# Seven products of quarters in place of eight for a 512-row channel matmul, with the sums on VectorE and GpSimd

## The chip, the cores and the metric

The kernel runs on one core of a Trainium2 chip. The metric is device time in microseconds (us), the median over executions.

Five engines take part. TensorE ("PE" in the profile) multiplies, and its weight loads have a line of their own ("PEld"). VectorE ("DVE"), ScalarE ("ACT") and GpSimd ("POOL") work element by element. SyncE ("SP") does nothing here but issue transfers, which run on 16 DMA engines. Each engine has its own queue of instructions; in these traces it works through it in order (group 3 below shows sums on VectorE that stand behind an operation which waits for a load). SBUF is the on-chip memory, and PSUM the one that TensorE's products go to.

## The reference

```python
# q, k, v: (8 batches, 8 heads, 576 rows, 64), float32
theta = pi / 2 * arange(576) / 576
phi(x) = concat([relu(x) * cos(theta), relu(x) * sin(theta)], axis=-1)     # 128 features
kv  = einsum('bhsf,bhsd->bhfd', phi(k), v);   z = phi(k).sum(axis=2)
x   = einsum('bhsf,bhfd->bhsd', phi(q), kv) / (einsum('bhsf,bhf->bhs', phi(q), z) + 1e-6)
x   = x as (8, 576, 512)
u   = x + (relu(x^T @ w_tok1) @ w_tok2)^T          # tokens: 576 -> 256 -> 576
out = u + relu(u @ w_ch1) @ w_ch2                  # channels: 512 -> 1536 -> 512
```

The last line is the largest part. The change concerns its second product, `relu(u @ w_ch1) @ w_ch2`.

## The kernel before

All inputs of the matmuls are bf16, sums on TensorE are fp32. The rows of the channel part are worked on in 8 "groups" of 512 rows that matter here, one per batch for batches 1 to 7 (g = 1..7), and g = 8 for the tails, which are the last 64 rows of all eight batches. Batch 0 is done in the head of the kernel, which also casts weights and is not pipelined in this way.

In group g TensorE does 48 matmuls for the first channel product (12 tiles of `h1T`, 4 matmuls each), then 48 for the second (4 row tiles, 12 matmuls each). Each is 128x128 weights against 512 columns.

```python
def mlp1(g, mi):                      # first channel matmul, one of 12 tiles
    ps = nextM()
    for ki in range(NCC):             # 4
        nc.tensor.matmul(ps..., wc1[:, ki, mi*P:(mi+1)*P], src[:, :, ki, :], ...)
    return ps

def mlp2(g, t, part, ps, sub=(0, 4)):  # second channel matmul, a third of one row tile
    for ki in range(4 * part + sub[0], 4 * part + sub[1]):
        nc.tensor.matmul(ps, h1T[:, ki, t * P:(t + 1) * P], wc2[:, ki, :],
                         start=(ki == 0), stop=(ki == NCH - 1))

def mlp2_out(g, t, ps, last):
    nc.vector.tensor_add(r[:, t % 2, :], ps, group(g)[1][:, t, :])     # + u
    stores.append(lambda: store(g, t, r))
```

Between these 24 steps of a group the rest of the work is interleaved: attention and token part of batch b = g+1, and features of batch f = g+2, with the loads for the batch after that at the end.

```python
def plan_of(g):
    b, f = g + 1, g + 2
    ...                                       # [cut: g == 1 has its own plan]
    if b < B:
        for j in range(NJ):  put(2 + j, num_step, b, j)      # attention output, wants qpT
        for n in range(2):
            put(8 + n, b1_step, b, n)                        # token matmul 1
            put(11 + n, u_step, b, n)                        # token matmul 2, u, u's transpose (DMA)
        put(13, tail_step, b)
    if f < B:
        for j in range(NJ):
            put(7 + j, k_step, f, j)          # key features (VectorE, ScalarE), value cast (GpSimd)
            put(12 + 2 * j, q_step, f, j)     # query features, then a transpose by DMA into qpT
            put(18 + j, kv_step, f, j)        # k^T v on TensorE
    if f + 1 < B:
        put(NS - 1, loads_step, f + 1)        # k, v, q of one batch: 3.54 MB
```

Loads, the five query transposes and the two or three transposes of u in a group are all issued by SyncE, so they stand in one queue. The stores go through GpSimd's queue, those of the tails through SyncE's and ScalarE's.

Of the kernel before, what the change touches and what calls it, by code (L numbers as in the profile page):

```python
# [18 lines left out]
def kernel(  # L19
# [11 lines left out]
    nc = tc.nc  # L31
# [24 lines left out]
    def sb(name, shape, dt):  # L56
        return const.tile(shape, dt, name=name)
# [27 lines left out]
    h1T = sb("h1T", [P, NCH, 4 * P], BF16)  # L85
    res_all = sb("res", [P, 2, 2, Dm], F32)
    res = [res_all[:, i] for i in range(2)]
    wz = sb("wz", [P, 512], BF16)

    LO, HI = slice(0, P // 2), slice(P // 2, P)  # L90
    psM, psA = [], []
# [2 lines left out]
    def nextM():  # L94
        cnt["M"] += 1
        return psM[(cnt["M"] - 1) % 4]
# [3 lines left out]
        return psA[cnt["A"] % 2]  # L100


    def place(b, j):
        return j

    def load(b, src, name, engs, h0=0, h1=None):
        h1 = H if h1 is None else h1
        dst = raw[name][b % 2]
        s = src[b].rearrange("h (i n) d -> i h n d", n=9)
        parts = ((1, 5, 9, 0), (0, 0, 5, 0))  # L110
        for (par, lo, hi, at), eng in zip(parts, engs):
            eng.dma_start(out=dst[par:P:2, h0:h1, at:at + hi - lo, :], in_=s[:, h0:h1, lo:hi, :])


    def feat(eng, out_ap, in_ap, tab, j):
        s = tab[:, j:j + 1]
        if eng is nc.scalar:
            eng.activation(out_ap, in_ap, AF.Relu, bias=0.0, scale=s)  # L118
        else:
            eng.tensor_scalar(out_ap, in_ap, scalar1=s, scalar2=0.0, op0=ALU.mult, op1=ALU.max)  # L120

    def kfeat(b, j, e0, e1, h0=0, h1=H):
        src = raw["k"][b % 2][:, h0:h1, place(b, j), :]
        feat(e0, kp[j][:, h0:h1, 0, :], src, cos_t, j)
        feat(e1, kp[j][:, h0:h1, 1, :], src, sin_t, j)

    def qfeat(b, j, e0, e1, h0=0, h1=H):
        src = raw["q"][b % 2][:, h0:h1, place(b, j), :]
        feat(e0, qp[j][:, h0:h1, 0, :], src, cos_t, j)
        feat(e1, qp[j][:, h0:h1, 1, :], src, sin_t, j)  # L130

    def copy(eng, out_ap, in_ap):
        if eng is nc.scalar:
            eng.copy(out_ap, in_ap)
        else:
            eng.tensor_copy(out_ap, in_ap)  # L136

    def vcast(b, j, eng, h0=0, h1=H):
        copy(eng, vb[j][:, h0:h1, 0:D], raw["v"][b % 2][:, h0:h1, place(b, j), :])

    def qturn_dma(b, j):
        nc.sync.dma_start_transpose(out=qpT[:, :, j, :],
# [158 lines left out]
    def mlp1_part(g, mi, bank, kis):  # L301
        src = group(g)[0]
        for ki in kis:
            nc.tensor.matmul(bank.rearrange("p (t k) -> p t k", k=P), wc1[:, ki, mi * P:(mi + 1) * P],
                             src[:, :, ki, :], start=(ki == 0), stop=(ki == NCC - 1))
# [12 lines left out]
    def mlp2_out(g, t, ps, last):  # L318
        r = res[(t // 2) % 2]
        nc.vector.tensor_add(r[:, t % 2, :], ps, group(g)[1][:, t, :])  # L320
        stores.append(lambda: store(g, t, r))

    stores = []

    def flush():
# [31 lines left out]
                nc.tensor.transpose(t[:, i, h, :], qp[j][:, HH * hf + h, :, :].rearrange("p a d -> p (a d)"),  # L357
                                    ident)

    def turn_half_out(hf, js, bank, eng):  # L360
        t = bank.bitcast(BF16).rearrange("p (j h t) -> p j h t", j=2, h=HH)
        dst = qpT[:, HH * hf:HH * hf + HH, js[0]:js[0] + len(js), :].rearrange("p h j t -> p j h t")
        copy(eng, dst, t[:, 0:len(js), :, :])

    def kv_half(hf, j):
        ps = bank_kv(hf)
# [11 lines left out]
    def num_half(hf, js, ps):  # L378
        for i, j in enumerate(js):
            for h in range(HH):  # L380
                num_mm(ps[:, i, h * E1:(h + 1) * E1], HH * hf + h, j)

    def x_half(hf, js, ps, b, stages=(0, 1, 2)):
        m = len(js)
        n = ps[:, 0:m, 0:HH * E1].rearrange("p g (h e) -> p g h e", h=HH)
        r = rden[(js[0] // 2) % 2]
        rm = r[:, 0:m, :]
        if 0 in stages:
            nc.vector.tensor_scalar_add(rm, n[:, :, :, D], 1e-6)
        if 1 in stages:  # L390
            nc.vector.reciprocal(rm, rm)
        if 2 not in stages:
            return
        c0 = HH * D * hf
        if js[0] < T:
            dst = x_sb[:, js[0]:js[0] + m, c0:c0 + HH * D].rearrange("p g (h d) -> p g h d", h=HH)
        else:
            dst = x_tl[b % 2][:, c0:c0 + HH * D].rearrange("p (g h d) -> p g h d", g=1, h=HH)
        rb = bass.AP(tensor=r.tensor, offset=r.offset, ap=[r.ap[0], [HH, m], [1, HH], [0, D]])
        nc.vector.tensor_mul(dst, n[:, :, :, 0:D], rb)  # L400

    def b1_half(hf, js, bank, b):
        c0 = HH * D * hf
        for j in js:
            for mi in range(NT):
                ks = slice(0, P) if j < T else LO
                rhs = x_sb[:, j, c0:c0 + HH * D] if j < T else x_tl[b % 2][LO, c0:c0 + HH * D]
                nc.tensor.matmul(bank[:, mi * 256:(mi + 1) * 256], w1[ks, j, mi * P:(mi + 1) * P], rhs,  # L408
                                 start=(j == 0 and mi == 0), stop=(j == NJ - 1 and mi == NT - 1),
                                 skip_group_check=True)  # L410
# [23 lines left out]
    def uT_out(b, c, bank, eng):  # L434
        copy(eng, uT[b % 2][:, :, c, :], bank.rearrange("p (t k) -> p t k", t=T))
# [112 lines left out]
    def turn(hf, i):  # L548
        turn_half(hf, pairs[i], psT[i % 2])

    def turn_o(hf, i, eng):
        turn_half_out(hf, pairs[i], psT[i % 2], eng)

    warm(12)
    for j in range(NJ):
# [33 lines left out]
        kv_half(1, j)  # L589
    turn(1, 1)  # L590
    kv_half_out(1, A)
    turn_o(1, 1, A)
    turn(1, 2)
    turn_o(1, 2, V)
    w1_cast(0, 2, G)
# [5 lines left out]
        wc1_cast(mi, G)  # L601
    for i in range(2):
        num_half(1, pairs[i], num_b[i])
    for st in range(3):
        for i in range(2):
            x_half(1, pairs[i], num_b[i], 0, (st,))
    b1_half(0, range(NJ), psK[0], 0)
    b1_half_out(0, psK[0], 0, A)
    num_half(1, pairs[2], num_b[2])
    x_half(1, pairs[2], num_b[2], 0)  # L610
    for c in range(2):
        uT_x(c, psT[c])
    b1_half(1, (0, 1), psK[1], 0)
    for c in range(2):
        uT_h(0, c, psT[c])
        uT_out(0, c, psT[c], A)
    b1_half(1, (2, 3, 4), psK[1], 0)
    b1_half_out(1, psK[1], 0, V, 0)
    b1_half_out(1, psK[1], 0, A, 1)
    bank_u = {2: psK[0], 3: psN[1][:, 0, :]}  # L620
    bank_h = {0: psT[0], 1: psT[1], 2: psN[0][:, 0, :], 3: psN[0][:, 1, :]}
    for c in (2, 3):
        uT_x(c, bank_u[c])
    for mi in (0, 1):
        mlp1_part(0, mi, bank_h[mi], (0, 1))
    for c in (2, 3):
        uT_h(0, c, bank_u[c])
        uT_out(0, c, bank_u[c], (A, V)[c - 2])
    for mi in (2, 3):
        mlp1_part(0, mi, bank_h[mi], (0, 1))  # L630
    for mi in (0, 1):
# [21 lines left out]


    def f1k(b, j, which, eng):
        feat(eng, kp[j][:, :, which, :], raw["k"][b % 2][:, :, place(b, j), :], (cos_t, sin_t)[which], j)

    for j in range(NJ):
        vcast(1, j, G)
# [85 lines left out]
        load(3, src_of[n], n, (SY, SY))  # L745


    NS = 24

    def kv_step(b, j):  # L750
        kv(b, j)
# [40 lines left out]
    def plan_of(g):  # L792
        b, f = g + 1, g + 2
        plan = [[] for _ in range(NS)]

        def put(s, fn, *args):
            plan[s].append(lambda: fn(*args))

        if g == 1:
            put(5, tail_step, 1)  # L800
            put(13, tail_turn, 1)
            for j in range(NJ):
                put(j // 2 + 1, f1k, b, j, 0, V)
                put((j + 1) // 2 + 2, kv_step, b, j)
                put(5 + j, num_step, b, j)
            put(3, u_out, 1, 1)
            for n in range(2):
                put(11 + n, b1_step, b, n)
                put(14 + n, u_step, b, n)
            for j in range(NJ):  # L810
                put(8 + j, k_step, f, j)
                put(18 + j, kv_step, f, j)
            for j, at in enumerate((12, 13, 16, 17, 18)):
                put(at, q_step, f, j)
            put(NS - 1, loads_step, 4)
            return plan
        if b < B:
            for j in range(NJ):
                put(2 + j, num_step, b, j)
            for n in range(2):  # L820
                put(8 + n, b1_step, b, n)
                put(11 + n, u_step, b, n)
            put(13, tail_step, b)
        if f < B:
            for j in range(NJ):
                put(7 + j, k_step, f, j)
                put(12 + 2 * j, q_step, f, j)
                put(18 + j, kv_step, f, j)
        if f + 1 < B:
            put(NS - 1, loads_step, f + 1)  # L830
        return plan

    for g in range(1, B + 1):
        mps = {}
        plan = plan_of(g)
        for s in range(NS):
            if s < NCH:
                ps = mlp1(g, s)
            else:
                t, part = divmod(s - NCH, 3)  # L840
                if part == 0:
                    mps[t] = nextM()
                mlp2(g, t, part, mps[t])
            for fn in plan[s]:
                fn()
            flush()
            if s < NCH:
                mlp1_out(s, ps, V if s in (7, 9, 11) else A)
            elif part == 2:
                mlp2_out(g, t, mps[t], g == B)  # L850

    flush()
    _ = tile, bass_utils
# [30 lines left out]
```

## Time and profile before

The median was 274.08 us (3 runs, 273.56 to 274.92).

A stretch from the first channel matmul of one group to that of the next: this is the windows view. Its columns are the stretch in us, its length, then the busy us and number of instructions of PE, PEld, DVE, ACT and POOL, then the granted clock, the busy share of the 16 DMA engines, and the GB/s that they moved. The rows are groups 1, 2, 3, 6 and 7.

```profile
57.50:86.90 29.40, 29.29 (x246) 14.56 (x245) 21.34 (x43) 16.29 (x26) 5.79 (x10) 1.00 0.85 233
86.90:114.90 28.00, 27.97 (x207) 13.52 (x208) 16.57 (x35) 15.70 (x25) 6.30 (x11) 1.00 0.88 228
114.90:142.10 27.20, 27.20 (x203) 13.34 (x202) 16.45 (x34) 15.04 (x24) 5.25 (x9) 1.00 0.89 237
...
197.30:224.10 26.80, 26.80 (x168) 12.27 (x167) 12.89 (x25) 9.11 (x15) 3.40 (x6) 1.00 0.38 96
224.10:244.80 20.70, 20.70 (x98) 9.38 (x97) 4.84 (x7) 5.37 (x9) 2.15 (x4) 1.00 0.13 52
```

In groups 1 to 5 (4 and 5, left out, have 0.95 and 0.87) TensorE is full and the DMA engines are at 0.85 to 0.95.

Two more readings were used for the prediction. From the timeline, first the five key features of group 1 alone, and then how such a feature runs while GpSimd is casting:

```profile
59.07 2.15 DVE L120 TENSOR_SCALAR kp<-k_raw,cos_t 128x512 bf16<-128x512 f32 x5
71.29 3.41 POOL L136 CAST vb<-v_raw 128x512 bf16<-128x512 f32 x5 [11.89 <-DMA v_raw<-in_v_dram]
71.47 0.71 DVE L120 TENSOR_SCALAR kp<-k_raw,cos_t 128x512 bf16<-128x512 f32 x1
```

The feature takes 0.43 us a piece alone (2.15 for five) and 0.71 when a GpSimd cast is under way. And from the chain of waits, the second channel product of group 7, 48 matmuls in 10.36 us (215.9 ns a piece):

```profile
234.59 10.36 PE psM L315 x48
```

### The profile page before, as it was taken

To read this page: it belongs to the slowest core of one execution; us is meant where nothing else is said; L and a number is where in the kernel's file an instruction comes from. 1 tells how busy PE (TensorE), PEld (TensorE's weight loads), DVE (VectorE), ACT (ScalarE), POOL (GpSimd) and SP (SyncE) were. 2 spreads that over 40 slices of the span, in tenths; PEclk is the share of its full clock that TensorE was granted. 3 is DMA by queue.
4 is the path that set the end of the run, shared out by engine and by line. 5 is a ranking of instruction groups with operands and counts; after the bars stand their busy time and mean duration, and the time that the engine had idled before them with its cause. 6 is when DMAs were issued, how large, how long until landed. Compare 5 with 4: busy or idle time off the path is not lost.

```text
span 270.6 us, 4991 instructions
## 1 busy us (share of the span) xinstructions
PE 259.8 (96%) x1878; PEld 127.6 (47%) x1878; DVE 150.4 (56%) x330; ACT 136.1 (50%) x223; POOL 66.7 (25%) x130
## 2 busy tenths in 40 slices
PE   7689999999999999999999999999999999999992
PEld 2465465445445544554455445544554444444440
DVE  5872856796982658366836684477446531331331
ACT  4763685874673666354745474547553405204300
POOL 4195647160401222110412041104120011011000
PEclk9999999999999999999999999999999999999999
DMA  6999999999849993999499969996890051011022
GB/s 206 368 376 391 385 393 372 257 221 331 271 89 244 274 358 70 207 242 356 148 200 211 356 187 202 219 353 190 183 216 2 22 153 79 2 78 78 0 79 80
DMA packets 79480, 57.15 MB, mean 211 GB/s; under 512 B 48224, under 2 KB 73952, under 8 KB 79456
## 3 DMA queue, kind: packets, MB, share of 16 engines
q1 hardware_dynamic: 76032, 47.39, 63.7%
q0 software_dynamic: 2560, 8.39, 9.2%
q10 hardware_dynamic: 864, 1.05, 1.2%
q8 instruction: 15, 0.25, 0.4%
q14 instruction: 9, 0.07, 0.1%
HBM read 35.85 MB, written 9.44 MB: 167 GB/s over the span
## 4 chain that ended last, share of the span: by engine, by line
PE 87%; DVE 5%; DMA 4%; ACT 1%; issue 1%; SPq 0%; DVEq 0%
PE psM L297 34%; PE psM L315 31%; PE psA L235 5%; PE psA L213 5%; PE psA L163 3%; PE psA L182 3%; DMA k_raw<-in_k_dram 2%; DMA uT<-u_bf 2%; PE psA L186 1%; PE psK L408 1%; PE psA L217 1%; PE psA L276 1%; DVE res L320 1%; DVE qp L120 1%; PE psA L149 1%
## 5 line engine op out<-in xcount | busy, mean ns | idle before, releaser
L315 PE MATMUL psM<-w_ch,h1T 128*128 128x512 bf16 x432 | 102.2, 379 | 0.0
L297 PE MATMUL psM<-uT,w_ch 128*128 128x512 bf16 x368 | 88.0, 379 | 0.7 <-DVE res L320 0.5
L309 ACT ACTIVATE h1T<-psM 128x512 bf16<-128x512 f32 x77 | 45.8, 596 | 52.1 <-PE psM L297 50.8
L315 PEld LDWEIGHTS <-h1T 128*128 128x128 bf16 x432 | 39.7, 97 | 43.9 <-issue 1.5
L297 PEld LDWEIGHTS <-w_ch 128*128 128x128 bf16 x416 | 37.8, 97 | 42.6 <-issue 2.5
L320 DVE TENSOR_TENSOR res<-psM,u_sb 128x512 f32<-128x512 f32 x32 | 22.0, 689 | 38.0 <-PE psM L315 38.0
L136 POOL CAST vb<-v_raw 128x512 bf16<-128x512 f32 (+1 forms) x43 | 24.3, 609 | 58.7 <-DMA v_raw<-in_v_dram 49.2
L118 ACT ACTIVATE kp<-k_raw,sin_t 128x512 bf16<-128x512 f32 (+1 forms) x45 | 28.1, 667 | 14.1 <-DMA k_raw<-in_k_dram 14.1
L334 POOL DMA_DIRECT2D out_dram<-res x16 | 9.0, 563 | 90.8 <-DVE res L320 90.8
L311 DVE TENSOR_SCALAR h1T<-psM 128x512 bf16<-128x512 f32 x27 | 18.5, 683 | 20.3 <-PE psM L297 20.3
L120 DVE TENSOR_SCALAR kp<-k_raw,cos_t 128x512 bf16<-128x512 f32 (+1 forms) x45 | 20.9, 500 | 9.6 <-DMA k_raw<-in_k_dram 9.6
L118 ACT ACTIVATE qp<-q_raw,sin_t 128x512 bf16<-128x512 f32 (+1 forms) x40 | 24.9, 678 | 0.0
L240 DVE TENSOR_TENSOR u_sb<-psA,x_sb 128x1024 f32<-128x1024 f32 x16 | 19.5, 1216 | 9.8 <-PE psA L235 9.8
L203 DVE TENSOR_TENSOR x_sb<-psA,rden 128x512 bf16<-128x512 f32 x28 | 19.4, 691 | 1.0
L245 ACT CAST u_bf<-u_sb 128x1024 bf16<-128x1024 f32 x12 | 12.5, 1046 | 11.8 <-DVE u_sb L240 9.1
L120 DVE TENSOR_SCALAR qp<-q_raw,cos_t 128x512 bf16<-128x512 f32 (+1 forms) x40 | 16.4, 445 | 2.0 <-DMA q_raw<-in_q_dram 2.0
L235 PE MATMUL psA<-B,w_tok 128*128 128x512 bf16 x64 | 16.4, 379 | 0.0
L163 PEld LDWEIGHTS <-kp 128*128 128x128 bf16 x280 | 12.4, 98 | 6.8
L182 PEld LDWEIGHTS <-qpT 128*128 128x128 bf16 x256 | 11.8, 98 | 8.2 <-issue 1.4
L173 ACT CAST kv_sb<-psA 128x520 bf16<-128x520 f32 x7 | 4.2, 603 | 21.0 <-PE psA L163 21.0
L213 PE MATMUL psA<-x_sb,w_tok 128*128 128x512 bf16 x56 | 14.4, 379 | 0.0
L163 PE MATMUL psA<-vb,kp 128*128 128x65 bf16 x280 | 13.3, 193 | 0.0
(108 smaller groups left out, 198.1 us busy)
## 6 DMA issues: line engine op xcount, KB each, us to landing
out_dram<-res POOLq DMA_DIRECT2D x32, 256.0 KB, 3.7
k_raw<-in_k_dram SPq DMA_DIRECT2D x7, 640.0 KB, 8.3
v_raw<-in_v_dram SPq DMA_DIRECT2D x7, 640.0 KB, 9.8
q_raw<-in_q_dram SPq DMA_DIRECT2D x7, 640.0 KB, 9.8
k_raw<-in_k_dram SPq DMA_DIRECT2D x7, 512.0 KB, 7.2
v_raw<-in_v_dram SPq DMA_DIRECT2D x7, 512.0 KB, 9.1
q_raw<-in_q_dram SPq DMA_DIRECT2D x7, 512.0 KB, 10.6
u_sb<-in_moe_w_ch_dram SPq DMA_DIRECT2D x2, 1024.0 KB, 10.3
```

The lines of the kernel that those rows point to most:

```text
L118: eng.activation(out_ap, in_ap, AF.Relu, bias=0.0, scale=s)
L120: eng.tensor_scalar(out_ap, in_ap, scalar1=s, scalar2=0.0, op0=ALU.mult, op1=ALU.max)
L136: eng.tensor_copy(out_ap, in_ap)
L163: nc.tensor.matmul(ps[:, h // HH, (h % HH) * E1:(h % HH + 1) * E1], kp[j][:, h, :, :].rearrange("p a d -> p (a d)"), vb[j][:, h, 0:E1], st ...
L182: nc.tensor.matmul(dst, qpT[:, h, j, :], kv_sb[:, h, 0:E1], start=True, stop=True, skip_group_check=True)
L213: nc.tensor.matmul(ps[mi], w1[:, j, mi * P:(mi + 1) * P], x_sb[:, j, :], start=(mi == 0 and j == 0), stop=(mi == 1 and j == T - 1), skip_g ...
L235: nc.tensor.matmul(ps[:, half, :], w2[:, ki, 2 * c + half, :], B1[b % 2][:, ki, :], start=(ki == 0), stop=(ki == NT - 1))
L240: nc.vector.tensor_add(u_sb[b % 2][:, 2 * c:2 * c + 2, :], ps, x_sb[:, 2 * c:2 * c + 2, :])
L297: nc.tensor.matmul(ps.rearrange("p (t k) -> p t k", k=P), wc1[:, ki, mi * P:(mi + 1) * P], src[:, :, ki, :], start=(ki == 0), stop=(ki == ...
L309: eng.activation(h1T[:, mi, :], ps, AF.Relu)
L315: nc.tensor.matmul(ps, h1T[:, ki, t * P:(t + 1) * P], wc2[:, ki, :], start=(ki == 0), stop=(ki == NCH - 1))
L320: nc.vector.tensor_add(r[:, t % 2, :], ps, group(g)[1][:, t, :])
```

## The change

One group's second product is a 512 x 1536 matrix A (`h1T`) times a 1536 x 512 matrix B (`w_ch2`). Cut into quarters, A11 A12 / A21 A22 and B11 B12 / B21 B22, it takes eight products of quarters. Strassen's scheme in Winograd's form takes seven, at the price of sums of quarters before and after. TensorE's work for the second product falls from 48 x 512 to 84 x 256 columns, by an eighth. The sums are these:

- T1 to T4, four sums of weight quarters, 128x1536 each, once, on GpSimd before group 1.
- S1 to S4, four sums of activation quarters per group, in four pieces each, on VectorE, between the first product and the second.
- Joining the seven products: six adds from PSUM on VectorE, three adds on GpSimd and one copy on ScalarE per group, in place of four adds on VectorE.

There was no free SBUF for S1 to S4. They live in the second buffers of the raw inputs, so that from batch 4 on the raw inputs have one buffer instead of two. The plan of steps is spread out to make room on VectorE, and parts of the head are reordered.

```diff
+    def rawt(name, b):
+        return raw[name][b % 2 if b < 4 else 0]

+    def t_sums(eng):
+        eng.tensor_sub(T1, B12, B11)
+        eng.tensor_sub(T3, B22, B12)
+        eng.tensor_sub(T2, B22, T1)
+        eng.tensor_sub(T4, B21, T2)

+    def s_sums(g, c0, c1, eng):
+        [cut: views of the chunks c0 to c1]
+        eng.tensor_add(S1, A21, A22)
+        eng.tensor_sub(S2, S1, A11)
+        eng.tensor_sub(S3, A11, A21)
+        eng.tensor_sub(S4, A12, S2)

+    def mlp2_unit(g, i):
+        pr, tt = divmod(i, 2)
+        a, w, bank = ((A11, B11, "A"), (S2, T2, "X"), (S3, T3, "F"), (S1, T1, "E"),     # [shortened]
+                      (A12, B21, "A"), (A22, T4, "F"), (S4, B22, "E"))[pr]
+        for c in range(NQ):            # 6
+            nc.tensor.matmul(m[tt][:, tt, :], a[:, c, tt * P:(tt + 1) * P], w[:, c, :], ...)

-    NS = 24
+    NS = NCH + 14
+    order1 = [0, 6, 1, 7, 2, 8, 3, 9, 4, 5, 10, 11]
+    t_sums(G)
 ...                                             in plan_of(g)
+        for at, (c0, c1) in ((9 if g == 1 else 7, (0, 2)), (10 if g == 1 else 9, (2, 4)), (11, (4, 5))):
+            put(at, s_sums, g, c0, c1, V)       # [and the last piece after step 11]
-                put(11 + n, u_step, b, n)
-            put(13, tail_step, b)
+                put(13 + 2 * n, u_step, b, n)
+            put(17, tail_step, b)
-                put(7 + j, k_step, f, j)
-                put(12 + 2 * j, q_step, f, j)
-                put(18 + j, kv_step, f, j)
+                put((7, 8, 9, 12, 13)[j], f1k, f, j, 0, V)
+                put((7, 8, 10, 12, 13)[j], f1k, f, j, 1, A)
+                put(7 + j, vcast, f, j, G)
+                put((12, 15, 17, 20, 22)[j], q_step, f, j)
+                put((20, 21, 22, 24, 25)[j], kv_step, f, j)
 [cut: mlp2_sums, which joins the products; the head's new order; wz as a view of another tile]
```

## The prediction

> **What bounds it now.** TensorE. The page gives PE 96% busy of a 270.6 us span, granted clock 1.00 in every window, and the chain of waits is 87% PE (34% first channel matmul, 31% second). In the chain 48 matmuls of 128x512 take 10.36 us, 215.9 ns each, with no gap; PE idles about 10 us, nearly all in the first 17. Groups 2 to 5 take 27.3 to 27.9 us and PE is busy for all of it; VectorE is busy 16.5 us of that, ScalarE 15.5, GpSimd 5 to 6 (windows view).
>
> **What changes.** Per group g = 1..8, 48 matmuls of 512 columns become 84 of 256. The trace has eight 128x256 matmuls in a row with a start-to-start of 108.3 ns; their weight loads keep up (65-column matmuls with a load each start every 30.5 ns). So 84 x 108.5 = 9.1 us against 10.36: 1.25 us less per group, 10 us in all. If nothing else moved: about 264.
>
> Added: 16 bf16 sums per group on VectorE, on the path between first and second matmul. No bf16 SBUF add is in the trace; the Trainium skill ("VectorE: DVE Perf Modes", the perf-mode tier table) has tensor_tensor at 2x at best in bf16, about (N/2+151)/0.96 ns, so an estimate of 0.42 us (512) and 0.29 us (256): 5.5 us per group. PSUM adds go from 4 to 6 of 0.69 us. VectorE comes to about 23 of 26 us, in order. GpSimd gets three 512-column fp32 adds per group and, in front of group 1, four 1536-column bf16 adds of weights.
>
> **Where it will bite.**
> 1. Groups 2 to 5: VectorE's queue has the key features (which wait for k_raw; it lands 10 to 11 us after the group starts, while PE reaches that step at 7.4 us) in front of most of the sums. From 10.8 us some 6.5 us of VectorE work precede the last sum; PE wants it at about 16.5 us. Value casts on GpSimd land in the same stretch. Loss 0.5 to 3 us a group; I take 1 each, 4 in all.
> 2. Group 1: the four weight sums start at about 57.7 us. The skill's page "GPSIMD Engine Reference", elementwise accounting, gives 4497 ns for 2048 elements, so an estimate of 3.3 us each, 13 us. In this trace a feature op that starts during a GpSimd cast ends 0.28 us after the cast ends (0.48 alone, 0.71 to 0.83 then), strictly alternating. The five key features of batch 2 sit in that stretch, and PE's kv matmuls wait for them: up to 9 us lost if each waits for one sum; I take 4 as a middle.
> 3. Groups 6 to 8 have a light VectorE: nearly the full gain, minus about 0.3 us for the last sums. The end is some 0.3 us shorter (half-size last add). Head reordered: 0.5 us gain.
>
> Sum: 274.1 - 10 - 0.5 + 4 + 4 + 0.4 = 272 us, 264 to 284. Faster by over 2% 0.33, within 2% 0.40, slower 0.27.
>
> **What would show it.** Second-matmul start-to-start near 108 ns; groups 7 and 8 each 1 us or more shorter; in the view of waits, PE on the sums (VectorE) and, in group 1, kv matmuls on kp; kp features of 3 us or more while GpSimd sums run; PE busy time lower by 9 to 10 us, but idle up.
>
> **What would make it wrong.** Weight loads not hidden behind 256 columns (no gain anywhere). GpSimd sums that do not hold up VectorE, and k_raw landing earlier: then 265. Both losses at their full size, with a clock drop in the gaps: 285.

## More of the kernel before

How the transfers of one group are laid out is in the timeline of SyncE's queue (start, duration, instruction). One row can hold several issues.

```profile
117.21 2.22 SPq L112 DMA_DIRECT2D k_raw<-in_k_dram  x2
...
132.29 3.75 SPq L250 DMA_TRANSPOSE uT<-u_bf  x2
136.20 8.86 SPq L142 DMA_TRANSPOSE qpT<-qp  x5
```

The loads go out 2 to 3 us into the group (117.21, against its start at 114.90). Then SyncE is silent for some 8 us while they land, and then all the transposes follow, up to the end of the group. The loads and the transposes overlap by some 4 us only: the last query transpose before these loads was issued at 115.89 us and landed at 121.52.

From the page of the kernel before: the span, busy time by engine, and the busy tenths of 40 equal slices of the span for PE and for the 16 DMA engines; the last line is the chain of work that ended last, by engine.

```profile
span 270.6 us, 4991 instructions
PE 259.8 (96%) x1878; PEld 127.6 (47%) x1878; DVE 150.4 (56%) x330; ACT 136.1 (50%) x223; POOL 66.7 (25%) x130
PE   7689999999999999999999999999999999999992
DMA  6999999999849993999499969996890051011022
PE 87%; DVE 5%; DMA 4%; ACT 1%; issue 1%; SPq 0%; DVEq 0%
```

TensorE never stops after the first 20 us, and 87% of the chain is TensorE. But the fourth line shows a second row of nines: the DMA engines are nearly full too, with one dip per group, up to about 200 us.

## The result, and the profile after

The changed kernel took 290.88 us (median of 4, 290.66 to 291.51), the kernel before, run again beside it, 273.82 (4 runs, 272.94 to 274.92). The ratio is 1.062, with a 95% interval of 1.058 to 1.067: 6% slower. It is outside the predicted range. A ratio here is the mean time of one kernel's fast runs over that of the other's fast runs of the same rounds, so it is not quite the ratio of the medians.

From the page of the changed kernel, the same parts as before, and the granted clock:

```profile
span 289.1 us, 5758 instructions
PE 256.4 (89%) x2148; PEld 157.4 (54%) x2166; DVE 212.1 (73%) x467; ACT 145.8 (50%) x241; POOL 111.8 (39%) x158
PE   6699999964999979897989888969899899999991
PEclk9799999996699999999999999999999999999997
DMA  6999999999106899389948994699599005203004
PE 51%; DVE 12%; DMA 11%; SPq 2%; ACT 1%; issue 1%; DVEq 0%; ACTq 0%
```

TensorE is busy 3.4 us less but idle 22 us more. There is a hole in the ninth and tenth slices (58 to 72 us); the clock falls to 0.6 in the tenth and eleventh, and the DMA engines stand idle in the eleventh and twelfth. Then there are small holes all along, up to about 240 us. The chain is now only 51% TensorE.

The windows view of the changed kernel, for the same groups:

```profile
59.20:97.00 37.80, 32.38 (x281) 19.45 (x282) 34.14 (x57) 17.70 (x29) 19.39 (x14) 0.86 0.56 155
97.00:127.00 30.00, 27.09 (x247) 16.86 (x246) 24.25 (x54) 16.75 (x27) 10.85 (x15) 1.00 0.81 215
127.00:156.60 29.60, 26.52 (x242) 16.72 (x241) 23.98 (x52) 16.15 (x26) 9.43 (x12) 1.00 0.83 219
...
216.90:243.80 26.90, 25.53 (x207) 15.81 (x206) 18.73 (x42) 10.96 (x17) 7.31 (x9) 1.00 0.45 95
243.80:263.30 19.50, 19.50 (x134) 12.89 (x132) 10.37 (x24) 6.56 (x11) 5.93 (x7) 1.00 0.14 55
```

Put side by side, all groups (us):

| stretch | before | after | difference |
|---|---|---|---|
| head, up to group 1 | 57.5 | 59.2 | +1.7 |
| group 1 | 29.4 | 37.8 | +8.4 |
| groups 2 to 5 | 110.4 | 119.9 | +9.5 |
| group 6 | 26.8 | 26.9 | +0.1 |
| group 7 | 20.7 | 19.5 | -1.2 |
| group 8 and the end | 25.8 | 25.8 | 0.0 |
| span | 270.6 | 289.1 | +18.5 |

The head is no matter of the change as far as these runs show. In runs of the experiments whose head is the old one, group 1 started anywhere from 57.5 to 59.7.

The matmuls themselves did what they should. From the chain of waits, group 7's second product is now 9.17 us; 84 matmuls of 256 columns take 109.2 ns each:

```profile
254.33 9.17 PE psM L374 x84
```

That is the gain of 1.2 us, and group 7 shows it in full. Group 8 gains it too, and gives it back: before, only two on each queue were left for the end; now the last eight are issued together, four on SyncE's queue and four on ScalarE's, and the end is 1.1 us longer. (In e2_Tonly and e11_beforeLoadsACT below, whose ending is the old one, the stretch from group 8 on takes 25.2 us and not 25.8, so this loss is known to half a microsecond or so.)

Now group 1. From the timeline, the first of the four weight sums (the last ends at 70.65) and the key features (x5 is five instructions in one row):

```profile
57.83 3.11 POOL L344 TENSOR_TENSOR w_ch_t<-w_ch 128x1536 bf16<-128x1536 bf16 x1
60.78 10.90 DVE L139 TENSOR_SCALAR kp<-k_raw,cos_t 128x512 bf16<-128x512 f32 x5
```

Five features that took 2.15 us take 10.90. Each gets its turn only when a GpSimd sum has ended, and TensorE stands waiting for them.

And groups 2 to 5. TensorE's largest waits in the changed kernel are these (who waited, for what; us in total, how often, longest). Before, no wait after the head was over 0.5 us.

```profile
PE psA L182 <- DVE kp L139: 5.2, 3, 2.8
PE psA L201 <- DMA qpT<-qp: 4.5, 3, 2.5
PE psA L205 <- DMA qpT<-qp: 3.4, 3, 1.4
PE psM L374 <- DVE k_raw L354: 3.3, 4, 1.0
```

The first is group 1. The others are of two kinds: attention outputs that wait for a transpose of the queries (a DMA), and second products that wait for S2 (which has the name `k_raw`, since it lives there). The chain of waits in the middle of group 3 shows how the two kinds hang together (some steps between are left out):

```profile
134.17 5.53 DMA k_raw<-in_k_dram
...
146.51 0.59 DVE k_raw L354
...
147.15 0.94 PE psM L374 x7
```

The keys of the next batch land at 139.7, which is 12.7 us into the group (127.0). VectorE stands waiting for them, because a key feature is next in its queue. Behind it stand S sums, and the last piece of S2 is done at 147.1, a microsecond after TensorE ran out of other work. The late keys are not all of it: GpSimd casts the values in the same stretch, and sums of 256 columns take up to 0.69 us there, against 0.28 alone. Five of them lose some 1.8 us in this way, more than that wait. From the timeline, the casts and one such sum:

```profile
143.80 3.16 POOL L155 CAST vb<-v_raw 128x512 bf16<-128x512 f32 x5 [14.65 <-DMA v_raw<-in_v_dram]
145.17 0.69 DVE L356 TENSOR_TENSOR v_raw<-h1T,k_raw 128x256 bf16<-128x256 bf16 x1
```

And why do the keys land so late? The queue of SyncE for the same group:

```profile
126.58 6.89 SPq L161 DMA_TRANSPOSE qpT<-qp  x3
133.52 1.28 SPq L131 DMA_DIRECT2D k_raw<-in_k_dram  x2
```

The load is issued 6.5 us into the group, behind three query transposes. In the kernel before it was 2.3 us. So, as this reading has it, the delay goes round: late loads make late features, these make late sums and late query transposes, and those make the next loads late.

### The profile page after: what moved, and what is told of

Same layout as the page of the kernel before. It is cut to its first block, busy times and chain, and to the rows that moved or that the text cites. A ratio compares the mean times of both kernels' runs of the same rounds, so it can differ in the third digit from the quotient of the medians.

```text
span 289.1 us, 5758 instructions
## 1 busy us (share of the span) xinstructions
PE 256.4 (89%) x2148; PEld 157.4 (54%) x2166; DVE 212.1 (73%) x467; ACT 145.8 (50%) x241; POOL 111.8 (39%) x158
## 3 DMA queue, kind: packets, MB, share of 16 engines
q10 hardware_dynamic: 864, 1.05, 1.1%
## 4 chain that ended last, share of the span: by engine, by line
PE 51%; DVE 12%; DMA 11%; SPq 2%; ACT 1%; issue 1%; DVEq 0%; ACTq 0%
PE psM L374 23%; PE psM L316 19%; DMA k_raw<-in_k_dram 6%; DVE kp L139 5%; DMA qpT<-qp 5%; PE psA L182 2%; PE psA L254 2%; DVE k_raw L354 2%; DVE k_raw L353 2%; PE psA L232 2%; DVE h1T L330 1%; DVE k_raw L355 1%; DVE v_raw L356 1%; PE psA L201 1%; PE psA L295 1%; SPq L131 1%
## 5 line engine op out<-in xcount | busy, mean ns | idle before, releaser
L328 ACT ACTIVATE h1T<-psM 128x512 bf16<-128x512 f32 x87 | 51.4, 597 | 50.0 <-PE psM L316 49.2
L394 POOL TENSOR_TENSOR res<-res,u_sb 128x512 f32<-128x512 f32 x14 | 18.4, 1332 | 51.2 <-DVE res L392 51.2
L137 ACT ACTIVATE kp<-k_raw,sin_t 128x512 bf16<-128x512 f32 (+1 forms) x45 | 28.6, 667 | 17.2 <-DMA k_raw<-in_k_dram 17.2
L139 DVE TENSOR_SCALAR kp<-k_raw,cos_t 128x512 bf16<-128x512 f32 (+1 forms) x45 | 29.6, 683 | 5.6 <-DMA k_raw<-in_k_dram 5.6
L374 PEld LDWEIGHTS <-h1T 128*128 128x128 bf16 x288 | 26.7, 98 | 8.2 <-DVE h1T L330 3.4
L137 ACT ACTIVATE qp<-q_raw,sin_t 128x512 bf16<-128x512 f32 (+1 forms) x40 | 25.4, 680 | 10.3 <-DMA q_raw<-in_q_dram 10.3
L374 PEld LDWEIGHTS <-k_raw 128*128 128x128 bf16 x252 | 24.1, 98 | 10.5 <-DVE k_raw L354 4.4
L374 PE MATMUL psM<-w_ch,h1T 128*128 128x256 bf16 x192 | 25.3, 273 | 2.3 <-DVE h1T L330 2.3
L374 PE MATMUL psM<-w_ch_t,k_raw 128*128 128x256 bf16 x162 | 20.7, 273 | 3.3 <-DVE k_raw L354 3.3
L218 DVE TENSOR_SCALAR rden<-psA 128x8 f32<-128x8 f32 x35 | 5.8, 164 | 22.9 <-PE psA L201 18.4
L139 DVE TENSOR_SCALAR qp<-q_raw,cos_t 128x512 bf16<-128x512 f32 (+1 forms) x40 | 20.9, 542 | 2.2 <-DMA q_raw<-in_q_dram 2.2
L259 DVE TENSOR_TENSOR u_sb<-psA,x_sb 128x1024 f32<-128x1024 f32 x16 | 19.4, 1212 | 0.6 <-PE psA L254 0.6
L353 DVE TENSOR_TENSOR k_raw<-h1T 128x512 bf16<-128x512 bf16 (+1 forms) x28 | 11.6, 415 | 8.5 <-ACT h1T L328 8.2
```

Source lines behind the costliest of these rows:

```text
L137: eng.activation(out_ap, in_ap, AF.Relu, bias=0.0, scale=s)
L139: eng.tensor_scalar(out_ap, in_ap, scalar1=s, scalar2=0.0, op0=ALU.mult, op1=ALU.max)
L259: nc.vector.tensor_add(u_sb[b % 2][:, 2 * c:2 * c + 2, :], ps, x_sb[:, 2 * c:2 * c + 2, :])
L328: eng.activation(h1T[:, mi, :], ps, AF.Relu)
L353: eng.tensor_add(S1, A21, A22)
L374: nc.tensor.matmul(m[tt][:, tt, :], a[:, c, tt * P:(tt + 1) * P], w[:, c, :], start=(pr < 4 and c == 0 and (tt == 0 or own)), stop=(c == N ...
```

## The experiments

Two theories of where the 18 us went, with the rivals that came up later:

- **A, group 1:** the four GpSimd sums shut VectorE out. Rival: VectorE's own new sums do it.
- **C, groups 2 to 5:** the S sums hold VectorE's queue up, and TensorE waits for it. Rival: the order and the number of the transfers, SyncE's queue and the DMA engines, hold the group at about 27 us, and the sums only add to it.

The expectations name theories by letters, and some name rivals not listed here; each says what it expects in numbers. The group table at the end of the section holds the lengths of all groups, so the text quotes only what decides.

### Group 1: where the weight sums run

**e1_tV**: the weight sums on VectorE, a few steps into group 1.

```diff
-    t_sums(G)
+            put(3, t_sums, V)          # in the plan of group 1
```

> The changed kernel with one edit: the four weight sums run on VectorE inside group 1, behind the key features of batch 2, and no longer on GpSimd ahead of it. Theory A (a GpSimd sum of 3.1 to 3.3 us shuts out VectorE's [...]feature ops for its whole length, and the first kv matmuls of group 1 wait for those): group 1 shrinks from 37.9 us to about 30, kp features there are back at 0.48 us, the total falls by 7 to 9 us to about 282 to 284. Rival B (the features were late for their data, or group 1 is long because of VectorE's new sums between the two channel matmuls): VectorE now has even more work in group 1, so the total stays within 2 us of 291.

**e2_Tonly**: the kernel before, with four GpSimd sums of the same size whose result nobody uses.

```diff
+    scr = sb("scr", [P, NCH // 2, Dm // 2], BF16)
+    [cut: names of the quarters]
+    G.tensor_sub(scr, B12, B11)
+    G.tensor_sub(scr, B22, B12)
+    G.tensor_sub(scr, B22, B11)
+    G.tensor_sub(scr, B21, B22)
```

> The kernel before, with only four GpSimd sums of the same shape in front of group 1, their result unused. Theory A: they alone cost 7 to 9 us, total about 281 to 283, all of it in group 1 (29.4 to about 38 us). Rival B: they are harmless beside an otherwise unchanged group, total about 274.

e1_tV took 283.09 us, ratio 1.035: 8 us better than the changed kernel. Group 1 fell from 37.8 to 31.7. e2_Tonly took 282.81, ratio 1.034; its group 1 rose from 29.4 to 40.4 (start to start), and no other group moved by over 0.4. So the four GpSimd sums, and nothing else, cost the old kernel 9 us or more. From the timelines, e1_tV and then e2_Tonly:

```profile
59.64 2.15 DVE L139 TENSOR_SCALAR kp<-k_raw,cos_t 128x512 bf16<-128x512 f32 x5
```

```profile
59.13 11.91 DVE L120 TENSOR_SCALAR kp<-k_raw,cos_t 128x512 bf16<-128x512 f32 x5
```

The features are back to 2.15 us in the one and at 11.91 in the other. The sum itself is three times quicker on VectorE (0.94 us against 3.10 in these two traces). Theory A is shown. It agrees with the Trainium skill, "SBUF — State Buffer" (section "SBUF: two separate sides"), which says that GpSimd and those VectorE instructions that need a second port share a pair of ports, and that whoever starts first holds it for the whole instruction; the longest single feature of the changed kernel took 3312 ns, as long as one GpSimd sum.

All further variants of the changed kernel start from e1_tV.

### Groups 2 to 5: the sums

**e3_noS** (wrong result): e1_tV without the S sums; the products read parts of `h1T` in their place, in the same shapes.

```diff
-        S1, S2, S3, S4 = s_views(g)
+        S1, S2 = h1T[:, 0:NQ, 2 * P:4 * P], h1T[:, 0:NQ, 0:2 * P]
+        S3, S4 = h1T[:, NQ:NCH, 0:2 * P], h1T[:, NQ:NCH, 2 * P:4 * P]
 ...
-            put(at, s_sums, g, c0, c1, V)
```

> As e1_tV, but without any of the sums of quarters of the activations on VectorE (the products read plain quarters; the result is wrong on purpose). Theory C (groups 2 to 5 are 2 to 3 us longer than before because these sums on VectorE, queued behind key features that wait for k_raw, come late): groups 2 to 5 fall to about 26 to 27 us, the total to 265 to 268. Rival D (they are longer because the inputs are now single-buffered and loaded late, or because the u step is later): they stay at 28 us or more, total 275 or more.

**e4_kLate**: the key features behind the sums in VectorE's queue, at steps 12 to 17 instead of 7 to 13, so that no sum can wait for a load.

```diff
-                put((7, 8, 9, 12, 13)[j], f1k, f, j, 0, V)
-                put((7, 8, 10, 12, 13)[j], f1k, f, j, 1, A)
+                put(12 + j, f1k, f, j, 0, V)
+                put((12, 13, 14, 16, 17)[j], f1k, f, j, 1, A)
```

> As e1_tV, but in groups 2 to 5 the key features stand behind the sums in the queues of VectorE and ScalarE (steps 12 to 17 and not 7 to 13). Theory C with the wait for k_raw as its main part: groups 2 to 5 shrink by 2 to 4 us each against e1_tV, the total by 8 to 12, to about 270 to 274. If it is the plain amount of work on VectorE that counts, and not the wait in front of it: less than 1 us a group.

e3_noS took 279.78 us (ratio 1.022): without any S sum it is still slower than the kernel before. e4_kLate took 285.33 (ratio 1.043), slower than e1_tV. Both expectations of theory C missed. Groups 2 to 5 together take 120.5 us in e1_tV and 118.3 in e3_noS. The sums alone are worth 2.2 us of the 10.1 that e1_tV is above the 110.4 of the kernel before. (These are single profiled executions, and the two executions of e3_noS are 2.7 us apart. The medians of the whole kernels give 3.3.) What TensorE waited for in e3_noS:

```profile
PE psA L201 <- DMA qpT<-qp: 7.7, 3, 3.7
```

With the sums gone, TensorE still waits for the transposes of the queries: 8.4 us on the two lines of the attention output together, against 7.7 in e1_tV. In e4_kLate the second products wait 5.5 us for VectorE's adds from PSUM, which now stand behind the features, and the attention output 6.0 us for qpT. So the rival had to be looked at: the transfers.

### Groups 2 to 5: the order of the transfers

If only the order in SyncE's queue were at fault, then an earlier load, or a queue of its own for the loads, would mend it.

**e5_q0late**: the first query transpose behind the transposes of u, at step 15 instead of 12 (and the second at 16 instead of 15).

```diff
-                put((12, 15, 17, 20, 22)[j], q_step, f, j)
+                put((15, 16, 17, 20, 22)[j], q_step, f, j)
```

> As e1_tV, but in groups 2 to 5 the first query step comes after both u steps (step 15, not 12), as in the kernel before. Theory E (the groups are held by a loop through the one in-order DMA queue of SyncE: loads of the next batch wait behind this group's eight transposes, the first query transpose waits for the loaded q, and the u transposes and the VectorE adds of the u step stand behind that query): groups 2 to 5 shrink from 28.8 to 30.9 us to about 27 to 28.5, the total from 283 to 274 to 278. Theory C (the sums on VectorE are the cost, their place in the queue aside): less than 1 us a group, total 280 or more.

**e6_kvEarly**: the loads of keys and values at step 16, in front of the later transposes.

```diff
-            put(NS - 1, loads_step, f + 1)
+            for n in "kv":
+                put(16, load, f + 1, src_of[n], n, (SY, SY))
+            put(NS - 1, load, f + 1, q, "q", (SY, SY))
```

> As e1_tV, but the loads of the next batch's keys and values are issued at step 16, right after the last read of their single buffers, and only the queries' load stays at the end of the group. Theory E: keys land at the start of the next group instead of 11 to 14 us into it, queries some 4 us earlier; the sums no longer wait behind key features, the query transposes no longer hold the u steps; groups 2 to 5 at 26.5 to 28.5 us, total 272 to 277. Theory C: total 280 or more. A third outcome, groups longer than in e1_tV, would mean that loads and transposes hinder one another when they run together.

**e7_both** is both of these edits, and **e8_noSboth** (wrong result) is e7_both without the S sums.

> Both edits of e5_q0late and e6_kvEarly. Theory E: groups 2 to 5 at 26.2 to 27.5 us (TensorE's own work is about 26.1), total 268 to 273. If the two edits attack the same wait the gain is that of the better one alone.

> As e7_both, but without the sums of the activation quarters (wrong on purpose). With theory E right this is the floor of the seven-product kernel: groups 2 to 5 at 26.1 to 26.5 us, total 265 to 268; the distance from e7_both to it is what the sums on VectorE still cost, expected 1 us a group or less.

All four were worse: 295.67, 307.77, 314.98 and 308.32 us (ratios 1.083, 1.127, 1.154, 1.129). In e5_q0late, whose transposes come later, the waits for qpT grow to 14.4 us in all. The line that explains e6_kvEarly is again TensorE's wait for the query transposes:

```profile
PE psA L201 <- DMA qpT<-qp: 29.8, 5, 8.2
```

The loads that were let in front pushed the transposes back. e8_noSboth shows that without sums the same order costs as much: 29.9 us on that line.

**e9_loadsACT**: all loads of batches 4 to 7 issued from ScalarE's queue, at steps 0, 2 and 4 of a group, so that they need not stand behind SyncE's transposes.

```diff
-            put(NS - 1, loads_step, f + 1)
+            for i, n in enumerate("kvq"):
+                put(2 * i, load, f, src_of[n], n, (A, A))
```

> As e1_tV, but the input loads of batches 4 to 7 are issued from ScalarE's DMA queue at steps 0, 2 and 4 of the group that uses them, so that transposes on SyncE's queue no longer stand behind loads, nor loads behind transposes. Theory F (in e1_tV the groups 2 to 5 are held by the one SyncE queue: about 15 us from the issue of the loads to the landing of q, then eight transposes, in strict order): groups 2 to 5 fall from about 30 to 26.5 to 28 us, waits of TensorE on query transposes nearly vanish, total 270 to 275. Rival G (the 16 DMA engines themselves are full, whichever queue feeds them): groups stay at 29 us or more, total 280 or more.

**e10_noSloadsACT** (wrong result) is the same without the S sums, **e12_loadsACTuEarly** is e9_loadsACT with the u steps back at 11 and 12, and **e11_beforeLoadsACT** is the control: the same edit to the kernel before, which has no new sums at all.

> As e9_loadsACT without the sums of the activation quarters (wrong on purpose). Theory F: the floor, groups 2 to 5 at 26.1 to 27 us, total 265 to 269; its distance to e9_loadsACT is the price of the sums once the queue is out of the way. Rival G: 28 us or more a group.

> The kernel before with the same move of the loads to ScalarE's queue, as a control. TensorE bounds it, so theory F expects no change beyond 0.5%: 272.5 to 275. A slower result would show what the six issues on ScalarE cost a group by themselves.

> As e9_loadsACT, with the two u steps of groups 2 to 6 at steps 11 and 12, as in the kernel before, ahead of the first query step. Theory F: the u transposes leave 2 to 3 us earlier and TensorE has the u products to do while VectorE finishes the sums: 0.3 to 1 us a group less than e9_loadsACT, total 267 to 273, perhaps the first correct version under the kernel before.

They took 309.61, 302.44, 307.48 (the control) and 305.19 us, ratios 1.131, 1.104, 1.123 and 1.114. The theory that SyncE's queue alone is the limit fell, and the control is why: the old kernel, with all its slack on VectorE, loses 12% by the same edit. Its largest wait, and how long a query transpose took from issue to landing there (the second line, from the view of that tile; in the kernel before it is 3.1/4.3/6.6):

```profile
PE psA L186 <- DMA qpT<-qp: 21.0, 4, 7.2
DMA to landing us min/median/max: 3.1/4.6/13.6
```

A transpose issued at 124.2 us, with loads in flight, landed at 136.6. So the loads and the transposes get into each other's way whichever queue issues them: in e6_kvEarly all of them are on SyncE's. The edit of the control changes the queue and also the moment of issue, and no run parts the two. The Trainium skill says in "Trainium Kernel Development and Optimization" (Key Constraints) that transfers from different queues "run on the same 16 DMA engines and interleave", and that a second queue only saves issue time. This agrees with the first (the transpose of 12.4 us stood in one queue, the loads in the other); no run shows the second by itself. The old order (loads, then silence, then transposes) is not slack. As far as e6_kvEarly and the control show, it is what keeps the landing times short.

By what arbitration the transposes come so late is open: the runs show when they were issued and when they landed, not why.

### Groups 2 to 5: how much the transfers bind

**h1_noV** (wrong result): e1_tV without the value loads of batches 4 to 7. **h2_noSnoV** (wrong result): e3_noS, the one without S sums, without them as well.

```diff
     def loads_step(b):
-        for n in "kvq":
+        for n in "kq":
```

> As e1_tV, but the values of batches 4 to 7 are not loaded (wrong result on purpose): one third less load traffic in groups 2 to 5, everything else as it was. Theory H (the DMA engines' loads and transposes are what holds groups 2 to 5): these groups fall from 28.8 to 30.9 us to about 26.5 to 28, the total from 283 to 270 to 277. Theory C (VectorE's sums hold them): 1 us a group or less, total 279 or more.

> As e3_noS without the values' loads of batches 4 to 7 (wrong on purpose). Theory H: groups 2 to 5 reach TensorE's own 26.1 to 26.6 us, total 264 to 268. If they stay at 27.5 or more, neither sums nor loads are the whole story.

**h5_before42** (wrong result): the kernel before with 42 of its 48 second-product matmuls in groups 1 to 8. It has TensorE's saving of the change without any of its costs: 6 x 215.9 ns = 1.3 us a group.

```diff
+            if g >= 1 and (ki == 5 or (ki == 6 and t < 2)):
+                continue
```

> The kernel before with 42 instead of 48 second-channel matmuls in groups 1 to 8 (wrong on purpose): 1.3 us less TensorE work a group, nothing added, order of everything else unchanged. If the DMA engines are a second limit just under TensorE (theory H in its full form), groups 7 and 8 fall from 20.7 to 19.4 us and group 6 by about 1.3, but groups 2 to 5 by less than 0.5 us each. If groups 2 to 5 fall to 26.0 to 26.6 too, total about 264, the old order had room for it and it is the new plan (u steps later, queries ahead of them, sums) that made the loop longer.

h1_noV took 277.13 us (ratio 1.012) and h2_noSnoV 272.19 (0.994). Groups 2 to 5 together:

| groups 2 to 5, us | with all loads | without value loads |
|---|---|---|
| with S sums | 120.5 (e1_tV) | 114.8 (h1_noV) |
| without S sums | 118.3 (e3_noS) | 108.7 (h2_noSnoV) |

The sums are worth 2.2 us and the loads 5.7 by themselves, and 11.8 together, 3.9 more than the two added. That would mean that the two costs interact, but it is not clear of the noise: by the medians of the whole kernels it is 3.3, 6.0 and 10.9, only 1.6 more, and the two executions of e3_noS differ by 2.7. Two more cautions: h1_noV and h2_noSnoV take away not only 1.2 of 3.5 MB, but also the GpSimd casts' wait for the values, and the query load's place behind them. The runs don't part these three.

From the windows view of h2_noSnoV, its group 3:

```profile
117.00:144.10 27.10, 26.22 (x242) 16.85 (x241) 17.48 (x36) 16.03 (x26) 9.16 (x13) 1.00 0.81 200
```

27.10 us, against 27.20 before, at a DMA share of 0.81. Over groups 2 to 5 this kernel is 1.7 us shorter than the one before (108.7 against 110.4), a third of the 4.8 that TensorE saves. What keeps the rest, with neither the sums nor a third of the loads there, is only partly seen: TensorE waits 2.5 us for qpT.

h5_before42 took 268.62 us, ratio 0.982 (interval 0.975 to 0.989). This is the run to look at closest, because it has no new sums anywhere. From its windows view, groups 2 to 4:

```profile
89.40:117.10 27.70, 26.73 (x200) 12.88 (x201) 16.06 (x34) 15.54 (x25) 5.84 (x10) 1.00 0.96 221
117.10:144.80 27.70, 26.19 (x197) 12.76 (x196) 16.12 (x34) 15.10 (x25) 5.24 (x9) 1.00 0.91 235
144.80:171.60 26.80, 26.79 (x201) 12.86 (x200) 16.72 (x35) 15.58 (x26) 6.47 (x11) 1.00 1.05 246
```

Group 7 is 1.3 us shorter (19.4 against 20.7), the whole saving. Groups 2 to 5 are together 1.4 us shorter (109.0 against 110.4), of 5.2 us that were taken from TensorE. The DMA engines are at 0.91 to 1.05 in these groups (the view's share can pass 1). The groups differ, though: group 3 is 0.5 us longer than before, and group 4, at the highest share of all, has nearly its whole saving (1.2 us, against the less than 0.5 expected). So the share alone does not tell where TensorE will wait. Waits appear that the kernel before did not have (a third, on L186 for qpT, is 1.0 us):

```profile
PE psA L182 <- DMA qpT<-qp: 2.0, 3, 1.5
PE psM L297 <- DMA uT<-u_bf: 1.7, 1, 1.7
```

So the transfers were a second limit, only a little below TensorE. One batch's loads (3.54 MB) keep all 16 engines busy for about 10.5 us in the trace, its eight transposes for 10 to 12, its stores for about 3.2: 24 to 26 us of a group of 27.2 to 28.0. That is an estimate added up from the trace. With these transfers in this order a matmul scheme has little to win there, however cheap its sums.

It is not the whole loss of the changed kernel. h5_before42 and e3_noS both have TensorE's saving and no S sums, and yet groups 2 to 5 take 109.0 us in the one and 118.3 in the other. These 9.3 us come from what else the change brought: the new order of steps, the single raw buffers, and the adds that join the products. TensorE's waits for qpT differ by 5.4 us (8.4 in e3_noS, 3.0 in h5_before42), and without the values' loads the groups come down to 108.7 (h2_noSnoV), so what is new seems to act through the transfers. What part each has is not shown: no run had the new order in the kernel before, or the old order under seven products in these groups. The one step towards the old order that was run, e5_q0late, made them longer (124.2 us).

### Where the change pays

**h3_last2** (correct): the kernel before, with seven products only in groups 7 and 8, which have no loads and little else. **h4_last3** (correct): in groups 6, 7 and 8. The weight sums run on GpSimd at the start of the group before, ahead of its key features (in h4_last3 from 167.8 to 177.2 us, and the keys land at 180.8); T3 is the last, since it overwrites a weight quarter. The raw inputs keep two buffers, as they are no longer loaded by then.

```diff
+    GS = 6                                          # h3_last2: 7
 ...
+        if g == GS - 1:
+            put(0, t_sums, G)                       # T1, T2, T4
+        if g >= GS:
+            if g == GS:
+                put(0, t3_sum, G)
+            for at, (c0, c1) in ((7, (0, 2)), (9, (2, 4)), (11, (4, 5))):
+                put(at, s_sums, g, c0, c1, V)
-                put(11 + n, u_step, b, n)
+                put((12, 13)[n] if g >= GS else 11 + n, u_step, b, n)
```

> The kernel before, with seven products only in groups 7 and 8 (no loads, no features there), weight sums on GpSimd in group 6[...]. Both groups were 19.5 us against 20.7 in every run so far: 2.4 us less than the kernel before in all, 271 to 272; ratio 0.989 to 0.993. If the weight sums or the head of group 7 cost something it shows in group 6 or 7 alone.

> The same with group 6 as well (no loads, but the last numerators and u step run there). Theory H: group 6 falls from 26.7 to about 25.5 us, what it was in e3_noS, if the sums fit; total 270 to 271.5. If the sums are late again, group 6 is at 26.6 as in e1_tV and h4 equals h3.

**h6_best** (correct): h4_last3 with the stores of the last row tile on GpSimd's queue, against the crowd of stores at the end.

```diff
-                eng = nc.sync if par else nc.scalar
+                eng = nc.gpsimd if t == 3 else nc.sync if par else nc.scalar
```

> As h4_last3, with the two stores of one of the last four tiles on GpSimd's queue, so that SyncE and ScalarE issue three instead of four each at the end. 0.3 to 0.7 us less than h4_last3: 270 to 271, ratio to before 0.985 to 0.990.

h3_last2 took 272.24 us (4 runs; kernel before 273.33), ratio 0.994, interval 0.988 to 1.000. h4_last3 took 271.21 (4 runs), ratio 0.989, interval 0.981 to 0.996. h6_best took 271.56 (6 runs; kernel before 273.21), ratio 0.994, interval 0.989 to 0.998: the stores on the third queue are not shown to help. From the windows view of h4_last3, groups 5 and 6:

```profile
171.80:199.10 27.30, 27.14 (x200) 13.42 (x202) 16.41 (x34) 15.31 (x25) 11.82 (x12) 1.00 0.87 232
199.10:224.90 25.80, 25.52 (x202) 15.77 (x202) 18.63 (x42) 10.16 (x17) 7.94 (x8) 1.00 0.39 81
```

Group 5 carries the GpSimd sums (11.82 us of POOL) and is as long as before. Groups 6 and 7 are 1.0 and 1.1 us shorter (25.8 and 19.6). With group 8 giving its gain back in the stores, some 2 us of the ten are to be had. The interval of h4_last3 leaves out 1.

The lengths of the groups in all runs (us, from first channel matmul to first channel matmul, of the profiled execution; "kernel" is the median of all executions):

| run | kernel | g1 | g2 | g3 | g4 | g5 | g6 | g7 |
|---|---|---|---|---|---|---|---|---|
| before | 273.82 | 29.4 | 28.0 | 27.2 | 28.0 | 27.2 | 26.8 | 20.7 |
| after | 290.88 | 37.8 | 30.0 | 29.6 | 30.1 | 30.2 | 26.9 | 19.5 |
| e1_tV | 283.09 | 31.7 | 28.8 | 30.1 | 30.9 | 30.7 | 26.6 | 19.5 |
| e2_Tonly | 282.81 | 40.4 | 27.9 | 27.3 | 28.1 | 27.3 | 27.2 | 20.7 |
| e3_noS | 279.78 | 29.8 | 27.4 | 31.5 | 28.6 | 30.8 | 25.5 | 19.5 |
| e4_kLate | 285.33 | 30.8 | 30.8 | 32.3 | 28.6 | 31.8 | 25.5 | 19.5 |
| e5_q0late | 295.67 | 31.3 | 29.1 | 31.4 | 31.2 | 32.5 | 32.4 | 19.5 |
| h1_noV | 277.13 | 30.6 | 29.7 | 27.9 | 29.0 | 28.2 | 26.6 | 19.5 |
| h2_noSnoV | 272.19 | 29.8 | 27.0 | 27.1 | 27.1 | 27.5 | 25.5 | 19.5 |
| h4_last3 | 271.21 | 29.5 | 27.9 | 27.3 | 27.9 | 27.3 | 25.8 | 19.6 |
| h5_before42 | 268.62 | 29.7 | 27.7 | 27.7 | 26.8 | 26.8 | 25.9 | 19.4 |

## Why the prediction was wrong

It said 272.0 us, 264 to 284, and the kernel takes 290.88. The steps, in its own terms:

1. **"10 us in all" from the matmuls: right.** It took 108.5 ns for a matmul of 256 columns; 109.2 were measured, 9.17 us for 84. Group 7 has the gain of 1.2 us. TensorE's busy time fell by 3.4 us only, not by the 9 to 10 forecast: in group 1, at a granted clock of 0.86, it rose by 3.1 (29.29 to 32.38). The durations of the sums were right too: 0.42 us (512 columns) and 0.28 to 0.29 (256) on VectorE where it ran alone, and 3.11 to 3.26 on GpSimd, so both estimates from the Trainium skill agree with this trace.
2. **"Group 1: ... I take 4 as a middle": the mechanism was right, the size was not.** The prediction said that the four GpSimd sums would shut VectorE out in turns, "up to 9 us lost". Its own figures (four sums of 3.3 us, five features, one turn each) gave the 9, and there was no reason for half. e2_Tonly shows 11.0 us for the sums alone (40.4 against 29.4). In the changed kernel the group is 8.4 longer although it gained 1.2, so it lost 9.6; of these, 6.1 go when the weight sums move to VectorE (37.8 to 31.7 in e1_tV). The clock in that group, 0.86, has a part in it; the prediction named such a drop as a risk and did not add it up.
3. **"Groups 2 to 5: ... Loss 0.5 to 3 us a group; I take 1 each": this is the step that failed most.** The net change was +2.0, +2.4, +2.1 and +3.0 us, so the loss was 3.2 to 4.2 us a group against the gain of 1.2, above the top of its own range. The path it gave, VectorE's queue with late keys in front of the sums, is in the trace (group 3 above), but it is not the main one: without any S sum (e3_noS) only 2.2 of 10.1 us go, and with the keys behind the sums (e4_kLate) groups 2 to 5 get longer, 123.5 us against 120.5. What TensorE waits for in its place is the transposes of the queries: 7.9 us in the changed kernel and 8.4 in e3_noS, where the kernel before had no such wait. The prediction left the transfers out of its sum. It took the landing of the keys, 10 to 11 us into the group, as a constant, and it moved to between 12.7 and 13.6. And it did not count the DMA engines: the windows view of the kernel before had them at 0.85 to 0.95 in just these groups. h5_before42 shows that even a free saving on TensorE is worth 1.4 of 5.2 us there. How the rest divides between the new order of steps, the single buffers and the joining adds stays open.
4. **"Groups 6 to 8 ... nearly the full gain": half right.** Group 7 gained 1.2. Group 6 gained nothing (26.8 to 26.9), because it started with transposes that were still late: the chain has 6.65 us of a query transpose at its start. In h4_last3, where group 5 is left alone, group 6 gains 1.0. Group 8 gained 1.2 and lost 1.1 at the end.
5. **"The end is some 0.3 us shorter": wrong.** It looked at the half-size last add, and not at the eight stores that all become ready within it.
6. **"Head reordered: 0.5 us gain": not seen.** The head was 1.7 us longer in the profile, but the unchanged head varies by 2.2 us from run to run (57.5 to 59.7).

Summed up, against the span: about 10.3 us too little loss in groups 2 to 5 (4 predicted, 14.3 measured), 5.6 in group 1 (4 predicted, 9.6 measured), some 2 in the head, and between 1 and 1.5 each in group 6 and at the end. That is the 20 us between a predicted -2 and a measured +18.5.

What stays open: why transposes land so late when loads are in flight; how much of the value loads' 5.7 us is their bytes and how much the casts; how much of the loss in groups 2 to 5 is the new order of steps; and whether the single raw buffers from batch 4 on add anything. The last is not visible in SyncE's waits (the three of over 1 us at the load line in the changed kernel, 1.8, 1.7 and 1.6, all fall in the head, and after it the longest is 0.4), but no run had two buffers with the sums in place, for lack of room. No correct version was found that gains in groups 1 to 5.

## What to carry to other kernels

When the engine that bounds a kernel is full, read the second row before you take work from it: here the DMA engines stood at 0.85 to 0.95 in the very groups where most of the gain was expected, and a free cut on TensorE was worth a quarter of its face value there. Apply such a change only where the rest of the machine has room (groups 6 to 8 here), and keep long GpSimd operations away from any stretch where something waits for VectorE operations that they shut out, as the key features here. A schedule in which loads, then transposes have the DMA engines nearly to themselves can look like slack; move a load into the gap on the unchanged kernel first, as a control, before you build on it.

## What the Trainium skill lacked or had wrong

- "DMA: Bandwidth & Descriptors" (Rules for kernel authors) says that a transpose next to ordinary DMAs "needs nothing". That concerns correct results, and every run here that should be correct was. For time it needs something: a query transpose lands 3.1 to 6.6 us after its issue in the kernel before, and up to 13.6 us with loads in flight (e11_beforeLoadsACT). No page gives the landing time of a transpose of this size (128x1024), or of any with loads beside it.
- "Advanced Engine Details and Errata" (X-Bar Transpose (TRN2)) says that transposes by DMA are as fast as regular DMAs. Here the eight transposes of a group, of 2 MB, took 10 to 12 us of all 16 engines in the trace, about as long as loads of 3.54 MB (10.5 us); an estimate from these numbers is some 180 GB/s against 340. The transposes go from SBUF to SBUF and the loads come from device memory, so the two are not alike in all else.
- "TensorE: Matmul & The Clock Gate" (Back-to-back issue gap) gives a sustained 131 ns for 512 columns and calls the formula N/2.4 + 2.5 too slow at that size. Here 48 matmuls in a row took 215.9 ns each, and 84 of 256 columns 109.2 ns, both as the formula says (215.8 and 109.2); nothing like the 131 of that section was seen.
- The lock on the shared ports is in the skill, but no page gives what a VectorE operation costs in a stretch where GpSimd runs short operations beside it. Here a VectorE sum of 256 columns took 0.28 us alone and up to 0.69 us beside value casts of 0.6 us each ("SBUF — State Buffer" would be the place).
